# Softmax weights times values: four heads side by side in the array, with value tiles that hold four heads and half of the tokens

## The chip, the cores and the metric

The kernel runs on one core of a Trainium2 chip. The metric is the device time of one execution in microseconds (us). The engines are named as in the profile: PE is the matmul engine and PEld its loads of stationary weights, DVE is VectorE, ACT is ScalarE, POOL is GpSimd, and SP is the queue that issues the DMAs.

## The reference, cut to what matters

Three stages follow each other: a landmark (Nystroem) attention over 4 batches of 8 heads with 576 tokens of 64 elements, a gated MLP, and a mixture of eight experts.

```
def _attn_ref(q, k, v):                      # q, k, v: (4, 8, 576, 64)
    q_lm = q.reshape(B, H, 32, 18, D).mean(axis=3)
    k_lm = k.reshape(B, H, 32, 18, D).mean(axis=3)
    A  = sm(q, k_lm); Bm = sm(q_lm, k_lm); C = sm(q_lm, k)
    Z = ... six Newton steps for the inverse of Bm ...
    return A @ Z @ C @ v
...
x = _moe_ref(attn_out, ...)      # rms norm, silu(x w_gate) * (x w_val), then w_out
return _moe2_ref(x, ...)         # skip score, gate, one expert of eight for each token
```

The change concerns one product, `C @ v`: for each head the 32 x 576 softmax weights of the landmarks times the 576 x 64 values, which gives 32 x 64 numbers for a head.

## The kernel before, in words

**Staging.** `attention(b)` runs once for each batch b = 0 to 3. It handles the 8 heads as two groups `hg` of four heads. A group's 4 x 32 landmark rows fill the 128 partitions, head h in partitions 32h to 32h+31. After the attention of a batch its 576 tokens go through the MLP as two units of 288 tokens (`run_unit`), and the attention of batch b+1 is spread over the units of batch b as a side generator. Batch 0 has nothing to run beside (`fast = True`, own pools with more buffers); there the conversion of the MLP's weights runs between its steps. The experts (`mixture`) come last.

**What sets the order.** The code is written as generators that yield, and a framework orders each engine's instructions from that when the program is built; the order is then fixed. So a small edit can move instructions on all engines. Each engine executes its own row in order, and waits on semaphores. A wait of the first instruction in a row holds up all behind it.

**The product.** In `group`, `load_v` brings values into a tile `vt` with 96 partitions: the 576 tokens are 32 landmarks x 3 thirds t x 6 tokens c, third t goes to partitions 32t to 32t+31, by three DMAs. `cT` holds the transposed softmax weights, 96 x 6 x 128. The product sums six matmuls c = 0 to 5 for each head into partitions 32h to 32h+31 of the PSUM tile `pv`. Its stationary operand is 96 x 32 (one head's weights), its moving operand is 96 x 64 (that head's values). Each such 32-bit float matmul is executed as two passes, so a head takes 12 passes and a group 48. Where four matmuls write to the four different quarters of the partitions, they use four different column tiles of the array (32 columns each). Before the change a value tile holds two heads with all six c, and the matmuls alternate between the two heads of a tile: 24 passes for the first pair of heads, then 24 for the second. For batch 0 both pairs have their own tile. For batches 1 to 3 there is a single `vt` buffer: the second pair's load starts after the first pair's matmuls, and other work stands between the two halves on PE. `A.activation(st["U"][:, hg], pv...)` reads the result.

**Names in rows.** `pv<-vt,cTs` is this product. `pv<-ap_t,P` is another thing: the value half of the MLP's first layer (`gemm`), as `pg<-ap_t,P` is its gate half; `o<-h_t,wo` is the MLP's projection. `P<-w..,WT` are the products that fold the attention's small matrix into the MLP weights (`product`, `product0`), `lp<-x2T,wcat` the logits, `sq<-T,bdq`, `sk<-T,bdk` and `pb<-lmk,bdq` the scores of a group, `bdq`, `bdk`, `T` and `s` what DVE prepares for them. `wo<-s,wo` and `wf` on DVE are conversions of 64-bit weights. `ap_t` is the attention output that the MLP multiplies, and `h` the hidden rows. Line 59 is a helper that all engines' instructions go through; line 248 is the DMA of `load_v`.

Of the kernel before, what the change touches and what calls it, by code (L numbers as in the profile page):

```python
# [6 lines left out]
F32 = mybir.dt.float32  # L7
# [8 lines left out]
B, H, S, D = 4, 8, 576, 64  # L16
# [47 lines left out]
def attention_moe_kernel(  # L64
# [4 lines left out]
    V, A, G, PE = (  # L69
        Paced(e, busy, n)  # L70
        for e, n in (
            (nc.vector, "V"), (nc.scalar, "A"), (nc.gpsimd, "G"), (nc.tensor, "P")
        )
    )
# [3 lines left out]
    def pool(stack, name, bufs=1, **kw):  # L78
        return stack.enter_context(tc.tile_pool(name=name, bufs=bufs, **kw))
# [36 lines left out]
    at = pool(pha, "at", side="right")  # L116
    sm = pool(pha, "sm", side="right")

    start, start1 = ExitStack(), ExitStack()
# [3 lines left out]
    fast = True  # L123
# [7 lines left out]
    def atbank(name):  # L131
        nonlocal nbank
        nbank += 1
        if fast and nbank % 4 < 2:
            return accbank(name)
        if fast and nbank % 4 == 2:
            return bank(name)
        return pa.tile([128, 512], F32, name=name, tag="a")
# [97 lines left out]
        r = st1.tile([128, 2, J * D], F32, name="kq", tag="raw")  # L236
        return {n: load_qk(0, hg, n, r[:, i]) for i, n in enumerate("kq")}

    def load_v(b, h0):
        if fast:  # L240
            vt = st0.tile([96, 2, 6, D], F32, name="vt", bufs=4)
        else:
            vt = at.tile([96, 2, 6, D], F32, name="vt")
        vv = v[b, h0 : h0 + 2].rearrange(
            "h (l t c) d -> t l h (c d)", t=3, c=6
        )
        for t in range(3):
            SP.dma_start(
                vt[32 * t : 32 * t + 32].rearrange("l h c d -> l h (c d)"), vv[t]
            )  # L250
        return vt

# [49 lines left out]
    def group(b, hg, st, loaded=None):  # L302
# [6 lines left out]
        for i, n in enumerate("kq"):  # L309
# [20 lines left out]
                mj.unsqueeze(1).unsqueeze(3).to_broadcast(shape), ALU.mult,  # L330
            )
            yield
        vt = load_v(b, 4 * hg)
        vt1 = load_v(b, 4 * hg + 2) if fast else None

        def two_halves(ps, lhs, rhs):
            for i in range(2):
# [45 lines left out]
        if fast:  # L383
            cT = st0.tile([96, 6, 128], F32, name="cTs", bufs=2)
        else:
            cT = at.tile([96, 6, 128], F32, name="cTs", tag="cG")
# [28 lines left out]
        (G if b in (1, 2) else V).tensor_tensor(eA, eA, b3(arec, L), ALU.mult)  # L415
        yield
        pv = atbank("pv")
        for p in range(2):
            if p:
                vt = vt1 or load_v(b, 4 * hg + 2)  # L420
            for c in range(6):
                for h in (2 * p, 2 * p + 1):
                    PE.matmul(
                        pv[32 * h : 32 * h + 32, 0:D],
                        cT[:, c, 32 * h : 32 * h + 32],
                        vt[:, h % 2, c, :],
                        start=(c == 0), stop=(c == 5),
                    )
        A.activation(st["U"][:, hg], pv[:, 0:D], AF.Copy, scale=crec)

        V.transpose(AT[:, hg], flat(eA))
# [130 lines left out]
    def attention(b, convs=()):  # L562
# [3 lines left out]
        if fast:  # L566
            loaded = [load_fast(hg) for hg in range(2)]
            gs = [group(b, hg, st, loaded[hg]) for hg in range(2)]

            def begin(hg):  # L570
                for _ in range(6):
                    next(gs[hg])
                    yield

            def left(hg):
                yield from inverse(st, hg, 1)

            yield from begin(0)
            ga = chain(begin(1), together(left(1), gs[1]))
            yield from together(ga, left(0), gs[0], convs)  # L580
            lhs, rhs = [st["X", g] for g in range(2)], [U[:, g] for g in range(2)]
        else:
            yield from chain(
                group(b, 0, st), group(b, 1, st), inverse(st, 0, 2, U)
            )
            lhs, rhs = ([st[n, g] for g in range(2)] for n in ("bm", "X"))
# [437 lines left out]
    def pair_at(lst, i):  # L1024
        return ld(lst, i, E - 1), ld(lst, i + LP, B - 1)
# [242 lines left out]
    fast = False  # L1268
# [45 lines left out]
    for u in range(1, 2 * B):  # L1314
        b, half = u // 2, u % 2
# [60 lines left out]
    with tc.For_i(0, npairs) as i:  # L1376
        e, b = pair_at(rest[0], i + 1)
# [36 lines left out]
```

## Time and profile before

| | |
|---|---|
| median of 3 runs | 689.48 us (687.76 to 691.85) |
| profiled execution, its own time | 689.0 us |
| its span (first to last instruction) | 687.3 us |
| mean granted clock of TensorE | 0.962 |
| busy: PE, PEld, DVE, ACT, POOL | 638.6, 552.4, 452.9, 275.1, 146.0 us |
| the product `pv<-vt,cTs` | 384 passes, starts from 23.9 to 389.0 us |

The busy times are of one profiled execution, and the 1.7 us between its span and its own time lie before the first and after the last instruction. An engine's share is an average: PE is nearly always busy after 86 us, and mostly waiting before.

### The profile page before, as it was taken

To read this page: it belongs to the slowest core of one execution; us is meant where nothing else is said; L and a number is where in the kernel's file an instruction comes from. 1 tells how busy PE (TensorE), PEld (TensorE's weight loads), DVE (VectorE), ACT (ScalarE), POOL (GpSimd) and SP (SyncE) were. 2 spreads that over 40 slices of the span, in tenths; PEclk is the share of its full clock that TensorE was granted. 3 is DMA by queue.
4 is the path that set the end of the run, shared out by engine and by line. 5 is a ranking of instruction groups with operands and counts; after the bars stand their busy time and mean duration, and the time that the engine had idled before them with its cause. 6 is when DMAs were issued, how large, how long until landed. Compare 5 with 4: busy or idle time off the path is not lost.

```text
span 687.3 us, 13145 instructions
## 1 busy us (share of the span) xinstructions
PE 638.6 (93%) x4831; PEld 552.4 (80%) x4831; DVE 452.9 (66%) x996; ACT 275.1 (40%) x613; POOL 146.0 (21%) x162
## 2 busy tenths in 40 slices
PE   5677499989999999999999998999999999999997
PEld 5456257977878987979889877999899988988985
DVE  5875899979879767988658867360645446353351
ACT  0652788534234522442531444340543235243240
POOL 4000025504200410320220221040453015032030
PEclk9755789999999999999999999999999999999999
DMA  8578475653249352339442217320552277553454
GB/s 287 197 277 272 178 244 185 199 152 88 53 139 210 74 139 93 62 98 219 102 93 70 70 35 168 98 36 1 152 137 100 43 225 228 163 173 142 138 153 161
DMA packets 111438, 97.16 MB, mean 141 GB/s; under 512 B 50064, under 2 KB 92048, under 8 KB 111376
## 3 DMA queue, kind: packets, MB, share of 16 engines
q1 hardware_dynamic: 111376, 96.34, 49.1%
q8 instruction: 38, 0.62, 0.4%
q14 instruction: 24, 0.20, 0.1%
HBM read 76.97 MB, written 19.34 MB: 140 GB/s over the span
## 4 chain that ended last, share of the span: by engine, by line
PE 66%; DVE 14%; DMA 6%; issue 5%; ACT 5%; POOL 2%; SPq 2%; DVEq 0%; ACTq 0%; POOLq 0%
PE o L59 17%; PE pv L59 10%; PE pg L59 9%; PE ph L59 9%; PE py L59 8%; PE P L59 3%; PE sq L59 2%; DVE wo L59 2%; PE nr L59 2%; PE sk L59 2%; DVE h L59 1%; ACT wo L59 1%; DMA x2r<-xT_d 1%; DVE s L59 1%; DVE T L59 1%
## 5 line engine op out<-in xcount | busy, mean ns | idle before, releaser
L59 PE MATMUL o<-h_t,wo 128*128 128x288 f32 x1152 | 165.9, 299 | 2.3 <-POOL h_t L59 1.4
L59 PEld LDWEIGHTS o<-h_t,wo 128*128 128x128 f32 x1152 | 155.7, 188 | 10.7 <-issue 6.3
L59 POOL TENSOR_TENSOR h_t<-h,h_t 128x288 fp32r<-128x288 f32 x96 | 83.7, 877 | 350.5 <-ACT h_t L59 327.9
L59 PE MATMUL pg<-ap_t,P 128*128 128x288 f32 x576 | 101.1, 304 | 11.1 <-ACT P L59 8.9
L59 PEld LDWEIGHTS pg<-ap_t,P 128*128 128x128 f32 x576 | 82.4, 189 | 25.1 <-issue 18.3
L59 PE MATMUL pv<-ap_t,P 128*128 128x288 f32 x576 | 98.6, 301 | 1.6 <-DVE h L59 1.3
L59 PEld LDWEIGHTS pv<-ap_t,P 128*128 128x128 f32 x576 | 82.7, 188 | 5.3 <-DVE h L59 2.3
L59 PE MATMUL ph<-xsh,P 128*128 128x288 f32 x384 | 78.1, 297 | 0.8 <-DVE P L59 0.8
L59 DVE SCALAR_TENSOR_TENSOR h<-h,pg 128x288 f32<-128x288 f32 x96 | 42.4, 447 | 33.6 <-ACT h L59 33.1
L59 PEld LDWEIGHTS ph<-xsh,P 128*128 128x128 f32 x384 | 62.0, 188 | 1.6 <-ACT P L59 1.0
L59 ACT ACTIVATE h<-pg 128x288 f32<-128x288 f32 x96 | 39.4, 412 | 44.5 <-PE pg L59 44.0
L59 PE MATMUL ph<-xsl,P 128*128 128x288 f32 x192 | 56.8, 296 | 0.0
L59 ACT CAST h_t<-h 128x288 fp32r<-128x288 f32 x96 | 41.2, 431 | 33.9 <-DVE h L59 33.8
L59 PE MATMUL py<-wo,h_t 128*128 128x512 f32 x210 | 51.8, 396 | 0.0
L59 PEld LDWEIGHTS py<-wo,h_t 128*128 128x128 f32 x210 | 39.6, 188 | 9.7
L59 DVE TENSOR_TENSOR h<-h,pv 128x288 f32<-128x288 f32 x96 | 42.5, 447 | 4.8 <-PE pv L59 0.6
L59 DVE STREAM_TRANSPOSE T<-kq 64x576 f32<-64x576 f32 (+1 forms) x40 | 35.5, 888 | 5.7 <-DMA kq<-in_k_dram 4.0
L59 ACT CAST P<-P 128x512 fp32r<-128x512 f32 x48 | 26.6, 586 | 26.9 <-PE P L59 24.9
L59 POOL TENSOR_TENSOR P<-w1r,P 128x512 fp32r<-128x512 f32 x16 | 20.7, 1293 | 74.7 <-ACT P L59 74.7
L59 PEld LDWEIGHTS ph<-xsl,P 128*128 128x128 f32 x192 | 36.2, 188 | 0.1
L59 DVE TENSOR_TENSOR P<-P,P 128x512 fp32r<-128x512 f32 x48 | 31.7, 680 | 4.8 <-ACT P L59 4.7
L59 DVE SCALAR_TENSOR_TENSOR h_t<-ph,h_t 128x288 fp32r<-128x288 f32 (+2 forms) x45 | 14.6, 353 | 28.5 <-ACT h_t L59 28.5
(220 smaller groups left out, 895.6 us busy)
## 6 DMA issues: line engine op xcount, KB each, us to landing
wl<-wg_d SPq DMA_DIRECT2D x36, 256.0 KB, 4.7
wr<-wv_d SPq DMA_DIRECT2D x32, 256.0 KB, 4.9
w1r<-in_moe_w_dram SPq DMA_DIRECT2D x32, 256.0 KB, 3.3
wr<-in_moe_w_gate_dram SPq DMA_DIRECT2D x6, 1024.0 KB, 8.1
wr<-in_moe_w_val_dram SPq DMA_DIRECT2D x6, 1024.0 KB, 5.9
wo<-in_moe_w_dram SPq DMA_DIRECT2D x24, 256.0 KB, 5.2
kq<-in_k_dram SPq DMA_DIRECT2D x8, 576.0 KB, 4.6
kq<-in_q_dram SPq DMA_DIRECT2D x8, 576.0 KB, 4.5
```

The source lines that it names most:

```text
L59: return f(*args, **kw)
```

## The change

The loops over the product are exchanged. All four heads of a group stand in the inner loop, so four consecutive matmuls go to the four column tiles. For batches 1 to 3 a value tile now holds all four heads with three of the six c; it has the same size as before, is still a single buffer, and the second load still follows the first half of the matmuls, now in front of c = 3. Its DMAs copy runs of 192 elements (768 bytes) where there were 384 (1536 bytes), twice as many of them. For batch 0 the tiles stay as they were (two heads each).

```
-    def load_v(b, h0):
+    def load_v(b, hg, i):
         if fast:
             vt = st0.tile([96, 2, 6, D], F32, name="vt", bufs=4)
         else:
-            vt = at.tile([96, 2, 6, D], F32, name="vt")
-        vv = v[b, h0 : h0 + 2].rearrange(
-            "h (l t c) d -> t l h (c d)", t=3, c=6
-        )
+            vt = at.tile([96, 4, 3, D], F32, name="vt")
+        n, m = vt.shape[1], vt.shape[2] * D
+        h0, d0 = (4 * hg + 2 * i, 0) if fast else (4 * hg, m * i)
+        vv = v[b, h0 : h0 + n].rearrange("h (l t c) d -> t l h (c d)", t=3, c=6)
         for t in range(3):
             SP.dma_start(
-                vt[32 * t : 32 * t + 32].rearrange("l h c d -> l h (c d)"), vv[t]
+                vt[32 * t : 32 * t + 32].rearrange("l h c d -> l h (c d)"),
+                vv[t][:, :, d0 : d0 + m],
             )
         return vt
...
-        vt = load_v(b, 4 * hg)
-        vt1 = load_v(b, 4 * hg + 2) if fast else None
+        vt = [load_v(b, hg, i) for i in range(2 if fast else 1)]
...
-        for p in range(2):
-            if p:
-                vt = vt1 or load_v(b, 4 * hg + 2)
-            for c in range(6):
-                for h in (2 * p, 2 * p + 1):
-                    PE.matmul(
-                        pv[32 * h : 32 * h + 32, 0:D],
-                        cT[:, c, 32 * h : 32 * h + 32],
-                        vt[:, h % 2, c, :],
-                        start=(c == 0), stop=(c == 5),
-                    )
+        for c in range(6):
+            if c == 3 and not fast:
+                vt.append(load_v(b, hg, 1))
+            for h in range(4):
+                PE.matmul(
+                    pv[32 * h : 32 * h + 32, 0:D],
+                    cT[:, c, 32 * h : 32 * h + 32],
+                    vt[h // 2][:, h % 2, c] if fast else vt[c // 3][:, h, c % 3],
+                    start=(c == 0), stop=(c == 5),
+                )
```

The framework's order moves with it. A row below counts matmuls, not passes, so a half of a group is x12. The first piece is PE in the second group of batch 0 (lines with - are of before, with + of the change).

```order
 L59 MATMUL nr<-Rb 128x128
-L59 MATMUL pv<-vt,cTs 32x64 x12
+L59 MATMUL pv<-vt,cTs 32x64 x2
 L59 MATMUL nu<-X,Rb 128x32 x2
 L59 MATMUL pG<-U,blk 128x64
 L59 MATMUL nu<-X,Rb 128x32
-L59 MATMUL pv<-vt,cTs 32x64 x12
+L59 MATMUL pv<-vt,cTs 32x64 x22
 L59 MATMUL pG<-U,blk 128x64
```

Of the 24 matmuls, 22 now stand behind the step that half of them stood behind; the two in front are heads 0 and 1 of c = 0.

The second piece is PE where the projection `o` of the first unit ends and the attention of batch 1 begins.

```order
+L59 MATMUL pg<-ap_t,P_662 128x288 x6
+L59 MATMUL pv<-ap_t,P_662 128x288 x3
 L59 MATMUL pb<-lmk_1308,bdq 128x32 x2
 L59 MATMUL sq<-T,bdq 128x288 x4
-L59 MATMUL pg<-ap_t,P_662 128x288 x6
-L59 MATMUL pv<-ap_t,P_662 128x288 x5
```

Nine matmuls of the next MLP unit have moved from behind the scores `pb` and `sq` to in front of them.

The third piece is DVE at the end of batch 0's attention, where the first `ap_t` is made.

```order
 L59 SCALAR_TENSOR_TENSOR wo<-s_839,wo 128x1024
 L59 TENSOR_TENSOR ap<-AT,rbs 128x288 x4
-L59 SCALAR_TENSOR_TENSOR wo<-s_839,wo 128x1024
 L59 TENSOR_TENSOR ap_t<-ap,ap_t 128x288 x4
 L59 TENSOR_TENSOR P_662<-P,P_662 128x512 x2
+L59 SCALAR_TENSOR_TENSOR wo<-s_839,wo 128x1024
 L59 SCALAR_TENSOR_TENSOR wo<-s_918,wo 128x1024
```

One weight conversion has moved from in front of the four `ap_t` rows to behind them and two rows of `P`.

## Rows read from the trace of the kernel before

**Rows 1.** The page, parts 1 and 2: busy times, and TensorE's clock in 40 slices.

```profile
PE 638.6 (93%) x4831; PEld 552.4 (80%) x4831; DVE 452.9 (66%) x996; ACT 275.1 (40%) x613; POOL 146.0 (21%) x162
PEclk9755789999999999999999999999999999999999
```

**Rows 2.** Everything on `vt`: shortest, median and longest pass in ns, then the span of starts.

```profile
L59 PE MATMUL pv<-vt,cTs x384: 218/219/316, 23.9 to 389.0; 96*32 96x64 f32 x192
```

**Rows 3.** Timeline of the product's blocks: start us, length us, engine, group.

```profile
23.90 1.35 PE L59 MATMUL pv<-vt,cTs 96*32 96x64 f32 x48
...
60.95 1.50 PE L59 MATMUL pv<-vt,cTs 96*32 96x64 f32 x24
...
250.15 0.86 PE L59 MATMUL pv<-vt,cTs 96*32 96x64 f32 x24
250.95 7.06 PE L59 MATMUL o<-h_t,wo 128*128 128x288 f32 x51
251.06 1.28 SPq L248 DMA_DIRECT2D vt<-in_v_dram  x3
...
257.94 0.86 PE L59 MATMUL pv<-vt,cTs 96*32 96x64 f32 x24
```

**Rows 4.** `vt` passes in flight in two stretches of 0.20 us, PE and PEld (busy, passes).

```profile
24.15:24.35 0.20, 0.20 (x14) 0.20 (x11) 1.00 0.00 0
24.36:24.56 0.20, 0.20 (x22) 0.20 (x18) 1.00 0.00 0
```

**Rows 5.** A product `P` on eight array tiles: timeline, then the passes' ns.

```profile
226.32 1.09 PE L59 MATMUL P<-wr,WT 64*32 64x256 f32 x32
...
L59 PE MATMUL P<-wr,WT x32: 376/376/400, 226.3 to 227.0; 64*32 64x256 f32 x32
```

**Rows 6.** Busy us (instructions) of PE, PEld, DVE, ACT, POOL by stretch; clock; DMA.

```profile
76.00:86.00 10.00, 1.08 (x6) 0.49 (x2) 10.00 (x13) 6.34 (x11) 0.00 (x0) 0.66 0.82 305
86.00:138.00 52.00, 50.94 (x315) 39.35 (x315) 49.25 (x76) 39.52 (x75) 20.86 (x18) 0.97 0.65 208
145.00:154.00 9.00, 9.00 (x80) 7.32 (x79) 6.35 (x14) 3.61 (x11) 0.79 (x1) 1.00 0.49 130
154.00:182.00 28.00, 25.47 (x219) 21.91 (x218) 26.64 (x74) 10.78 (x32) 9.01 (x10) 1.00 0.33 82
240.00:260.00 20.00, 20.00 (x183) 17.52 (x182) 12.60 (x26) 4.07 (x12) 2.61 (x3) 1.00 0.51 131
267.00:282.00 15.00, 14.64 (x143) 11.70 (x142) 12.50 (x41) 6.21 (x19) 3.53 (x4) 1.00 0.31 78
350.00:380.00 30.00, 30.00 (x259) 25.89 (x258) 22.22 (x58) 7.61 (x24) 1.61 (x2) 1.00 0.34 93
380.00:390.00 10.00, 10.00 (x114) 8.89 (x112) 8.62 (x24) 3.69 (x12) 2.94 (x3) 1.00 0.30 64
```

**Rows 7.** Timeline where DVE and PE wait for each other in batches 1 and 2.

```profile
142.52 0.63 PE L59 MATMUL pb<-lmk,bdq 128*128 128x32 f32 x4 [1.20 <-DVE bdq L59]
...
260.24 0.46 DVE L59 TENSOR_SCALAR x2T<-o 128x288 f32<-128x288 f32 x1 [2.09 <-PE o L59]
...
266.31 0.31 PE L59 MATMUL pb<-lmk,bdq 128*64 128x32 f32 x4 [0.51 <-DVE bdq L59]
```

**Rows 8.** Timeline around the first matmul of the first MLP unit.

```profile
82.77 1.22 DVE L59 SCALAR_TENSOR_TENSOR wo<-s,wo 128x1024 int32<-128x1024 int32 x1
...
83.91 1.56 DVE L59 TENSOR_TENSOR ap_t<-ap,ap_t 128x288 fp32r<-128x288 f32 x4
...
85.42 1.29 DVE L59 TENSOR_TENSOR P<-P,P 128x512 fp32r<-128x512 f32 x2
85.54 0.82 PE L59 MATMUL pg<-ap_t,P 128*128 128x288 f32 x2 [8.92 <-ACT P L59]
```

**Rows 9.** DMA issues between 140 and 400 us: count, size each, median us to landing.

```profile
wr<-wv_d SPq DMA_DIRECT2D x25, 256.0 KB, 4.9
vt<-in_v_dram SPq DMA_DIRECT2D x33, 96.0 KB, 2.3
```

**Rows 10.** The chain that ended last, its piece with the longest DMA before 150 us.

```profile
77.42 6.48 DMA wr<-in_moe_w_val_dram
```

## The prediction, made before the changed kernel was run

> **What bounds the kernel now.** I read the page's busy times first [rows 1]: PE is busy for 638.6 of 687.3 us, and its clock is granted at half in the slices before about 70 us and nearly in full after 100 us. So a matmul that gets shorter can count, but only where PE is what the others wait for. That is read by stretch [rows 6]. From 76 to 86 us PE is idle and DVE busy throughout. From 86 to 138 us both are full: PE 50.94 and DVE 49.25 of 52 us, the weight conversions running beside the first MLP unit. From 154 to 182 us, in the attention of batch 1, DVE is busy 26.64 of 28 us and PE 25.47: DVE leads and PE has the holes. From 240 to 260 (batch 2) and from 350 to 390 us (batch 3) PE has no hole at all.
>
> Then the product itself [rows 2, 3]. It has 384 passes in 8 groups. In batches 1 to 3 that is twelve blocks of 24 passes, each like the two shown, 0.86 us long. A pass takes 219 ns to its end (243 for the first), but passes overlap. A block has 12 rounds of two passes, one for each head of the pair; 0.86 less 0.24 for one pass, over the 11 steps from round to round, is 56 ns a round. At half clock the block of 1.50 us with its longest pass of 0.32 gives 107 ns, twice as much: the round is a number of cycles of this engine.
>
> **The change, step by step.**
>
> *The rounds.* With four heads in the inner loop a block has 6 rounds of four. What such a round takes is the disputed price. From below it is 56 ns: each column tile would still take its own 56 ns. From above it is 112 ns: four passes cost as much as twice two, and nothing is won. The trace holds a piece of the answer, since in batch 0's first group both pairs of heads stand directly behind each other. At two passes a round its 24 rounds would take 23 x 0.056 + 0.24 = 1.53 us; the block takes 1.35 [rows 3]. The time is missing at the change of pairs: a stretch of 0.20 us there has 22 passes in flight, an equal stretch before it 14 [rows 4]. So about three rounds ran with all four column tiles at work. The other near row is a product with eight array tiles [rows 5]: 32 passes of 0.38 us each in 1.09 us, or (1.09 - 0.38)/31 = 23 ns from pass to pass, with 256 columns in each where ours has 64. Issuing and loading weights for a pass therefore costs no more than 23 ns, and four cost at most 92; since those passes are paced by their columns, the real price is lower. I take 56 ns. A block then gets shorter by 6 x 56 = 0.336 us, and the twelve by 4.03 us of PE time. The upper end for issue, 92 ns, would leave 12 x (0.672 - 0.552) = 1.4 us.
>
> The Trainium skill (TensorE: Matmul & The Clock Gate, Part 3, Measured speedup vs the span model) reports 2.38 times the speed for three column tiles, which is 0.79 of full use. By that rule a round of four would cost an estimated 71 ns, and the twelve blocks would give 2.95 us instead of 4.03. With the same share of it kept as below, the result would be an estimated 685.8 us. The trace's stretch with 22 passes against 14 speaks neither clearly for the one nor for the other.
>
> *Batch 0.* The first group's block loses 12 rounds less the three it already saves, about 0.5 us, at 24 us, where PE goes on to wait for DVE and ACT; I count nothing. The second group: the order puts 2 matmuls first and 22 behind the step where the second half stood. Heads 2 and 3 still have 12 passes each in that block, and a column tile takes one a round, so its 12 rounds stay, and with them the 1.50 us. Nothing.
>
> *The transfers.* Three DMAs per load, as before, but with runs of 768 bytes. A load now lands 2.3 us after issue, and the three issues take 1.28 us, so the second half's data are there about 3.6 us after the first half [rows 3, 9]. The second half starts 257.94 - 251.01 = 6.9 us after the first ends, with gemm work in between; the order of the change keeps such work there. The bound from above for landing is that of 256 KB in runs of 1 KB, 4.9 us, which makes 6.2. Still hidden; uncovered by 1 us in each of six groups it would cost 6 us, for PE's row behind it waits.
>
> *What of the 4.03 us stays.* The four blocks of batch 3 lie where PE has no hole: all stays, 1.34 us. The first two of batch 2 lie before the wait of 0.51 us for `bdq` at 266.31. But DVE's work for `bdq` begins with a row that waited 2.09 us for PE's `o` [rows 7], so it comes earlier with PE: 0.67 us stays. Of the last two of batch 2, where DVE is busy 12.50 of 15 us [rows 6], I keep half, 0.34. In batch 1 DVE leads; I keep the last block only, 0.34. Sum 2.69 us, between 1.34 (batch 3 alone) and 4.03.
>
> *Moved work.* Nine matmuls of the next unit now stand before the scores of batch 1. PE was idle there for 1.20 us, waiting for `bdq` [rows 7]. The nine take about nine times 0.13 us (51 `o` passes in 7.06 us, the last one's length included) = 1.2 us, so they fit the hole. The hidden rows that DVE owes for them find room, since DVE is busy only 6.35 of the 9 us from 145 on [rows 6]. I count 1.2 us, between 0 (DVE gives it back by 182) and 1.5.
>
> On DVE the conversion of 1.22 us goes behind `ap_t`, so the first MLP matmul, for which PE sat idle 8.92 us, can start about 1.2 us sooner [rows 8]. But what follows is the stretch in which DVE is full, and its work is the same. I count 0, between 1.2 won and 2.5 lost (the conversion lands 1.22 + 1.29 us later).
>
> Sum: 689.0 - 2.7 - 1.2 = **685.1 us**. This goes against the profiled execution, 0.5 us under the median of the three runs.
>
> **The rivals.** *Absorbed.* The blocks do get shorter, but DVE's stretches and the reshuffled order take all back except batch 3: 689.0 - 1.3 = 687.7 us. For it: PE's holes in 154 to 182 are already larger than what batch 1 saves. Against: 240 to 260 has none.
>
> *No change in the array.* A round of four costs 112 ns. Then only the moved work counts: 689.0 - 1.2 = 687.8 us, or 689.0 without it. Against it stand the 22 passes.
>
> *More.* All twelve blocks count, the whole hole of batch 1 and the 1.2 us at 85 us: 689.0 - 4.0 - 1.5 - 1.2 = 682.3 us.
>
> *Slower: the conversions slip.* The displaced conversion is 2.5 us later on a DVE that is full until 138 us, and behind it stand the stores and the reuse of the raw buffers, whose next transfer was worth 6.48 us on the chain [rows 10]. If one such turn is missed, the first projection waits for its weights: 2.5 + 6.5 = 9.0 us lost against 2.7 won, 695.3 us. It decides from the point where the first scores of batch 1, now at 142.52 us, start more than 2.7 + 3.4 = 6.1 us later. Against it: DVE's total work is unchanged, and its rows go on without a gap.
>
> **How the numbers follow.** I give the forecast 0.50 (own range 683.5, with all twelve blocks and 1.5 us of the hole, to 687.1, with batch 3's blocks and half of the 1.2 us), *more* 0.12, *absorbed* 0.22, *no change in the array* 0.05 and *slower* 0.11. A measurement of this kernel tells about 0.5% from no change, 3.4 us, so faster means below 685.6. That takes in *more* and some two thirds of the forecast's range: 0.12 + 0.33 = 0.45. Slower is 0.11, the rest 0.44. The range goes from *more*, 682.3, to no change at all, 689.0; a little wider at the bottom for batch 0's 0.5 us: 681.8 to 689.0. Outside remain *slower* and a few hundredths.
>
> **What would show it.** A half of a group in batches 1 to 3 should be 0.86 - 0.34 = 0.52 us long, with as many passes; 0.86 would be *no change in the array*, and 0.62 to 0.75 an issue limit. The second block of batch 0 should keep about 1.5 us. PE's wait for `bdq` at the start of batch 1 should be gone, and the batch-1 scores should start within a microsecond of 142.5. The loads of `vt` should land within 2 to 3 us, and no second half should wait for them. The prediction is wrong if DVE's stretch from 154 to 182 us gets longer, or if the conversions end later than before.

## The result, and the profile after

| | before | after |
|---|---|---|
| median of the comparison's runs | 689.31 us (10 runs) | 693.48 us (10 runs) |
| ratio | | 1.0069, 95% interval 1.0045 to 1.0094 |
| span of the profiled execution | 687.3 us | 692.3 us |
| mean granted clock of TensorE | 0.962 | 0.956 |

The change made the kernel 0.7% slower; the forecast was 685.1 us, in a range of 681.8 to 689.0. The profile after shows at once that the array does what was forecast and that something else costs more. First two rows of the page of after.

```profile
PE 638.7 (92%) x4831; PEld 551.9 (80%) x4831; DVE 453.6 (66%) x996; ACT 274.4 (40%) x613; POOL 144.5 (21%) x162
PEclk9755799999999899999999999999999999999999
```

PE's busy time is that of before [rows 1], though its product got shorter, and TensorE's clock has a slice of 8 in the middle of what was a line of nines. The timeline of after, PE and DVE, at the places that the prediction spoke of and at three waits:

```profile
23.47 0.88 PE L59 MATMUL pv<-vt,cTs 96*32 96x64 f32 x48
...
60.69 1.50 PE L59 MATMUL pv<-vt,cTs 96*32 96x64 f32 x44
...
83.88 0.58 PE L59 MATMUL pg<-ap_t,P 128*128 128x288 f32 x1 [7.90 <-ACT P L59]
...
145.85 0.63 PE L59 MATMUL pb<-lmk,bdq 128*128 128x32 f32 x4 [0.41 <-DVE bdq L59]
...
160.10 0.44 DVE L59 SCALAR_TENSOR_TENSOR h<-h,pg 128x288 f32<-128x288 f32 x1
160.46 1.23 DVE L59 TENSOR_TENSOR bdk<-lmk,maskj 128x256 f32<-128x256 f32 x1
161.61 0.77 DVE L59 STREAM_TRANSPOSE AT<-sT 128x576 f32<-128x576 f32 x1
162.31 1.33 DVE L59 STREAM_TRANSPOSE T<-kq 128x1152 f32<-128x1152 f32 x1
163.57 0.41 DVE L59 TENSOR_TENSOR h<-h,pv 128x288 f32<-128x288 f32 x1
164.03 1.07 PE L59 MATMUL pv<-ap_t,P 128*128 128x288 f32 x6 [1.99 <-DVE h L59]
...
183.50 1.16 PE L59 MATMUL pg<-ap_t,P 128*128 128x288 f32 x6 [1.90 <-DVE h L59]
184.59 0.87 PE L59 MATMUL pv<-vt,cTs 96*32 96x64 f32 x24
...
227.85 0.69 PE L59 MATMUL lp<-x2T,wcat 128*32 128x288 f32 x8 [1.43 <-DVE P L59]
...
231.53 1.64 PE L59 MATMUL pg<-ap_t,P 128*128 128x288 f32 x6
...
259.11 0.54 PE L59 MATMUL pv<-vt,cTs 96*32 96x64 f32 x24
```

A half block takes 0.54 us where it took 0.86 [rows 3], and the first MLP matmul starts at 83.88 instead of 85.54 us [rows 8]. But the first scores of batch 1, `pb`, start at 145.85 instead of 142.52 us [rows 7]. PE then stands idle for 1.99, 1.90 and 1.43 us, each time for DVE. And two rows are odd: a half block of 0.87 us at 184.59, and six `pg` passes that take 1.64 us at 231.53, where six take 0.95 elsewhere. The windows around the last two waits say why (columns as in [rows 6], the clock is the eighth):

```profile
181.00:184.30 3.30, 1.40 (x11) 1.16 (x9) 2.65 (x8) 1.15 (x3) 0.51 (x1) 1.00 0.32 55
184.30:187.70 3.40, 3.40 (x37) 2.97 (x36) 2.45 (x6) 1.33 (x4) 2.20 (x3) 0.50 0.35 65
...
226.20:228.70 2.50, 1.07 (x11) 0.39 (x10) 1.60 (x3) 1.76 (x5) 0.79 (x1) 1.00 0.69 136
228.70:235.50 6.80, 6.80 (x31) 6.75 (x31) 3.60 (x13) 2.14 (x8) 1.59 (x2) 0.50 0.20 34
235.50:239.00 3.50, 3.50 (x51) 2.80 (x50) 2.53 (x9) 2.21 (x6) 0.80 (x1) 1.00 0.18 28
```

TensorE was granted half its clock, 1.2 instead of 2.4 GHz, for 3.4 and for 6.8 us, each time soon after one of the waits. Before had no such stretch between 90 and 686 us. Behind the first of the three waits the clock stayed full:

```profile
164.00:167.40 3.40, 3.37 (x22) 2.99 (x23) 3.40 (x9) 1.18 (x3) 1.56 (x2) 1.00 0.58 173
```

The other rows that the prediction named: the loads of `vt`, and DVE's splits of the products `P` from 89 to 122 us.

```profile
vt<-in_v_dram SPq DMA_DIRECT2D x33, 96.0 KB, 2.5
```

```profile
L59 DVE TENSOR_TENSOR P<-P,P 128x512 fp32r<-128x512 f32 x10 | 6.9, 690 | 2.5 <-ACT P L59 2.4
```

The loads land as forecast, in 2.5 us. DVE waited 2.5 us in front of the splits; the same view of before has 0.6 us.

### The profile page after: what moved, and what is told of

It is laid out like the page before. It is cut to its first block, busy times and chain, and to the rows that moved or that the text cites. A ratio compares the mean times of both kernels' runs of the same rounds, so it can differ in the third digit from the quotient of the medians.

```text
span 692.3 us, 13150 instructions
## 1 busy us (share of the span) xinstructions
PE 638.7 (92%) x4831; PEld 551.9 (80%) x4831; DVE 453.6 (66%) x996; ACT 274.4 (40%) x613; POOL 144.5 (21%) x162
## 4 chain that ended last, share of the span: by engine, by line
PE 72%; DVE 14%; DMA 5%; ACT 4%; issue 2%; POOL 1%; SPq 1%; ACTq 0%; POOLq 0%; DVEq 0%
PE o L59 16%; PE py L59 11%; PE ph L59 11%; PE pv L59 9%; PE pg L59 9%; PE P L59 3%; PE sq L59 3%; DVE wo L59 2%; PE nr L59 2%; DMA wl<-wg_d 2%; DVE T L59 2%; PE sk L59 1%; DMA kq<-in_q_dram 1%; DVE h L59 1%; DVE sT L59 1%
## 5 line engine op out<-in xcount | busy, mean ns | idle before, releaser
L59 POOL TENSOR_TENSOR h_t<-h,h_t 128x288 fp32r<-128x288 f32 x96 | 81.7, 854 | 355.1 <-ACT h_t L59 334.5
L59 PE MATMUL pv<-ap_t,P 128*128 128x288 f32 x576 | 102.0, 306 | 2.8 <-DVE h L59 2.8
L59 PEld LDWEIGHTS pg<-ap_t,P 128*128 128x128 f32 x576 | 84.2, 192 | 25.4 <-issue 16.7
L59 PEld LDWEIGHTS pv<-ap_t,P 128*128 128x128 f32 x576 | 84.6, 193 | 8.3 <-DVE h L59 4.0
```

What stands on the lines that cost most here:

```text
L59: return f(*args, **kw)
```

## The experiments

**How a kernel's order is held.** Both kernels write their instructions in the same sequence, up to the operands of one product. So the order in which the framework issues one kernel's rows can be laid on the other: an edge from each row of an engine to the next, which orders them and waits for nothing. The table says it in runs, first number + count, in the order of writing.

```
+ORDER = {
+    'PE': (
+        "0+9 11+5 9+2 16+8 25+2 24 27+10 39+24 37+2 63+3 67 73 66 71+2 68+3 74 76 85 "
...
+        for a, b in zip(want, want[1:]):
+            tc.add_manual_dep(
+                b, a.name,
+                mybir.DependencyInfo(
+                    mybir.DependencyClass.NoSync, mybir.DependencyReason.DATA
+                ),
+                reason="order",
+            )
```

The profiles are compared by three stretches, each from the first start of a matmul to the next, read off the timelines: A from `pG` of batch 0 (about 60 us) to the first `pb` of batch 1, B from there to the projection `o` of unit 2 (about 240 us), C from there to the last matmul. What lies ahead of A differs by up to 4 us between executions of whatever kernel, so this tells more than a single run's time. Each row's stretches are of one profile; in the kernels that were profiled twice, A and B differ by up to 0.9 us and C by up to 0.2. The ratio compares with runs of before in the same comparison, whose medians lie between 687.56 and 689.31 us, so times of different comparisons are compared by the ratio. "New" is the changed kernel's order, "wide" the changed product.

| run | order, product | us | ratio (95%) | A | B | C |
|---|---|---|---|---|---|---|
| before | old, pairs | 689.31 | | 82.66 | 97.36 | 442.41 |
| after | new, wide | 693.48 | 1.0069 (1.0045 to 1.0094) | 86.27 | 102.98 | 438.50 |
| after_again | the same | 693.15 | 1.0080 (1.0052 to 1.0108) | 85.69 | 103.72 | 438.31 |
| wide_oldorder | old, wide | 685.20 | 0.9959 (0.9934 to 0.9984) | 82.13 | 96.53 | 440.10 |
| pairs_neworder | new, pairs | 694.13 | 1.0089 (1.0054 to 1.0124) | 85.79 | 103.57 | 440.24 |
| halves_pairs_oldorder | old, halves in pairs | 686.88 | 0.9995 (0.9965 to 1.0024) | 83.34 | 96.81 | 440.82 |
| early_new | new to 141 us, wide | 690.42 | 1.0024 (0.9998 to 1.0049) | 85.06 | 98.41 | 441.40 |
| batch1_new | new 142 to 209 us, wide | 690.90 | 1.0044 (1.0014 to 1.0074) | 83.31 | 100.65 | 441.34 |
| unit2_new | new 209 to 240 us, wide | 685.45 | 0.9957 (0.9932 to 0.9982) | 82.12 | 96.63 | 439.85 |
| late_new | new from 240 us, wide | 683.81 | 0.9937 (0.9914 to 0.9960) | 82.29 | 96.65 | 438.10 |
| conversion_back | new but 80 to 89 us, wide | 694.85 | 1.0113 (1.0079 to 1.0146) | 86.75 | 100.75 | 438.43 |
| unit0_back | new but 89 to 141 us, wide | 692.18 | 1.0039 (1.0008 to 1.0071) | 83.54 | 103.81 | 437.83 |
| after_filled | new, wide, 1 wait filled | 692.11 | 1.0059 (1.0035 to 1.0084) | 85.45 | 100.77 | 438.29 |
| after_filled3 | new, wide, 3 waits filled | 687.91 | 1.0010 (0.9989 to 1.0031) | 86.02 | 98.95 | 437.92 |
| wide_b23 | framework's own, wide in batches 2 and 3 | 683.25 | 0.9940 (0.9909 to 0.9971) | 82.25 | 97.43 | 438.23 |
| wide_b23_again | the same | 685.87 | 0.9953 (0.9930 to 0.9976) | 83.16 | 97.40 | 438.17 |

### Product and order apart

Theories: *order* (the product gains what was forecast, the order of rows loses it), *tiles* (the new loads or four tiles at once cost), *absorbed*.

**wide_oldorder**: the changed kernel with the table of before.

> The changed passes and loads, with the rows of all five engines held in the order in which the kernel before has them (edges of order only, no waits). Theory 'order': the passes gain what they were forecast to gain and all of the loss is the new order of rows, so this is 685.3 to 686.7 us (2.7 to 4.0 under 689.3), a block is 0.52 us, the clock is granted in full from 90 us on without the two half stretches, and the first scores of batch 1 start within 1 us of 142.5. Theory 'tiles': the 768-byte loads, or four tiles side by side, cost other work time; then it is 692 to 694 us, as after. Theory 'absorbed': 688.5 to 689.3 us, the blocks being shorter but nothing of it left.

**pairs_neworder**: the kernel before with the table of the changed one.

> The passes and loads of the kernel before (heads in pairs), with the rows of all five engines held in the order in which the changed kernel has them. Theory 'order': 696.2 to 697.5 us, that is after's 693.5 plus the 2.7 to 4.0 us that the longer blocks cost; the first scores of batch 1 at about 146 us, and the clock granted at half near 184 and 229 us again. Theory 'tiles': about 689 us, as before, since the order alone costs nothing.

**halves_pairs_oldorder**: the changed tiles and loads, with this loop in batches 1 to 3, old order.

```
-        for c in range(6):
...
+        for i in range(2):
...
+            for p in range(2):
+                for c in range(6) if fast else range(3 * i, 3 * i + 3):
+                    for h in (2 * p, 2 * p + 1):
```

> Order of rows as before; tiles and loads of the change (four heads by half of the tokens), but in batches 1 to 3 within each half the heads in pairs, three rounds of two and three rounds of two, so never four side by side except where the pair changes; batch 0 in pairs as before. If the gain comes from four heads side by side: a half block of about 0.75 to 0.86 us and 688.5 to 689.5 us in all. If it came from the smaller loads or their place: as fast as the run with four side by side, 685 to 687 us. If the loads cost time: over 690 us.

**wide_b23**: old loads and loop in batches 0 and 1, nothing held.

```
+        new = b in (2, 3)
...
+        if new:
...
+        else:
+            for p in range(2):
```

> The change in batches 2 and 3 alone, order left to the framework: rows are as before until the second unit (about 216 us) and differ in about 340 of 3747 rows of TensorE behind it. Theory 'order', with the loss in batch 1 and at 216 to 240 us, where TensorE waits and its clock falls: 686.5 to 688 us (eight blocks of 0.34 us, less what the later rows give back), no half clock near 184 us. If new order costs wherever it comes: 689 to 691 us. Theory 'tiles': 691 to 692 us (two thirds of the loss).

*Order* holds. With the old order the product wins 0.41% of 689 us, 2.8 us (interval 1.1 to 4.5). The order alone, with the old product, costs 0.89%, 6.1 us. The old order's page and three rows of its timeline:

```profile
PE 634.3 (93%) x4831; PEld 547.6 (80%) x4831; DVE 451.9 (66%) x996; ACT 275.0 (40%) x613; POOL 145.8 (21%) x162
PEclk8755889999999999999999999999999999999999
```

```profile
158.06 0.77 DVE L200 STREAM_TRANSPOSE AT<-sT 128x576 f32<-128x576 f32 x1
158.75 0.41 DVE L200 TENSOR_TENSOR h<-h,pv 128x288 f32<-128x288 f32 x1
159.09 1.35 DVE L200 STREAM_TRANSPOSE T<-kq 128x1152 f32<-128x1152 f32 x1
...
230.87 0.97 PE L200 MATMUL pv<-ap_t,P 128*128 128x288 f32 x6
...
249.84 0.54 PE L200 MATMUL pv<-vt,cTs 96*32 96x64 f32 x24
```

PE is busy 4.3 us less than before [rows 1], batch 0's shorter blocks included, and the clock is full from 91 us on. pairs_neworder has the half clock at 184 and 229 us, so it comes with the order and not with the product. Its time came 2 us under the forecast, which had started from after's 693.5 us; in this comparison before, too, was 1.75 us faster than beside after. halves_pairs_oldorder has a surprise. Its half block is shorter than the 0.75 to 0.86 us expected:

```profile
247.62 0.68 PE L200 MATMUL pv<-vt,cTs 96*32 96x64 f32 x24
```

The likely reason: a half has its change of pairs in the middle, where rounds can overlap, as in batch 0 of before [rows 4]. Its stretches add up to 1.5 us less than before's, wide_oldorder's to 3.7 less; in the runs' times it can't be told from before, nor, by the intervals, from wide_oldorder. So in the blocks and stretches the gain goes with how many heads stand side by side, and no cost of the loads shows. wide_b23 came out 3 us faster than expected, and 0.6 us under the range in a second run.

### Where the order loses

Theories: *slip* (the displaced conversion makes DVE late, and what follows is a consequence) and *each place for itself*. The rows of the two orders differ in clusters with the same rows between them, so the table can take a stretch from one kernel and the rest from the other. The first line that each changes in DVE's table, against wide_oldorder's:

```
early_new
-"118+10 156+2 128+2 162 130 132 140 142 163 131 133 141 143 134+2 171 174 136 "
+"118+10 156+2 128+2 162 130 132 140 142 131 133 141 143 134+2 163 171 174 136 "
batch1_new
-"213 221 215 214 216+2 222 218 223 227 219 224 228 225 229 226 230+3 235 233+2 "
+"213 221 215 214 216+2 222 218 223 227 219 224 228 225 229 226 233 230 234 "
unit2_new
-"311+7 342 341 318 320 319 321 344 330 332 345 331 333 349+2 361+2 364 363 365 "
+"311+7 342 341 318 320 319 321 344 330 332 345 331 333 350 349 361+2 364 363 "
late_new
-"446 439 447+3 440 450 461 451+10 475 462+2 476 464 477+2 465 479 466 480+4 487 "
+"446 439 447+3 440 450+5 461 455+6 476+2 462+2 479 464 480+3 475 483 478 465 "
```

Number 163 is the displaced conversion.

> The changed passes; rows of all engines in the changed kernel's order up to about 141 us (batch 0, the first unit with its weight conversions), and behind that in the order of the kernel before. The run that had the old order throughout was 2.8 us faster than before. Theory 'slip' (the displaced conversion makes DVE late, and the rest of the loss follows from that): first scores of batch 1 about 3.3 us later than with the old order, and then most of the later loss too, holes in TensorE behind 160 us and the clock granted at half near 184 and 229 us: 690 to 693 us. Theory 'each place for itself': only the 3.3 us of this stretch, no half clock later: 688 to 689.5 us.

> The changed passes; the changed kernel's order in the attention of batch 1 alone (about 142 to 209 us), the old order ahead of it and behind it. Theory 'slip': the first scores start as with the old order, DVE is not late, and this stretch costs 0 to 1 us: 685 to 686.5 us, no half clock. Theory 'each place for itself': its own rows make the 2.2 us hole at 181 us and the half clock of 3.4 us behind it: 687 to 688 us.

> The changed passes; the changed kernel's order at the start of unit 2 alone (about 209 to 240 us), the old order elsewhere. Theory 'slip': 685 to 686 us, no half clock. Theory 'each place for itself': the order of DVE's rows there (the scaled probabilities of the second half and the split of the product ahead of the hidden rows) makes the hole ahead of the router's product and the half clock of 6.8 us behind it, 3 to 4.4 us: 688 to 690 us.

Neither theory as it stood. The first unit's rows cost A 2.9 us (85.06 against 82.13) and, with one half stretch, B 1.9. Batch 1's rows cost A 1.2 and B 4.1 us, without any slip ahead of them, which speaks against *slip*. Unit 2's rows alone, which *each place for itself* charged 3 to 4.4 us, cost nothing: PE's wait there was 1.11 us and the clock behind it full, where after has 1.43 us and a half stretch. In batch1_new both long waits stand as in after, and each has its half clock (windows of batch1_new):

```profile
158.80:162.10 3.30, 3.26 (x13) 3.26 (x14) 3.30 (x8) 1.17 (x3) 1.92 (x3) 0.50 0.60 179
179.30:182.60 3.30, 3.30 (x35) 2.85 (x35) 2.39 (x7) 1.48 (x4) 2.19 (x3) 0.50 0.32 55
425.10:428.40 3.30, 3.30 (x38) 2.08 (x39) 0.80 (x3) 1.07 (x2) 0.00 (x0) 0.50 0.03 8
```

The third lies in C, where the order is the old one; early_new has such a stretch at 427 us too. Both have a C some 1.3 us longer than wide_oldorder's, which has none there.

The first wait can be read in the DVE rows of after above. Between two rows of the MLP's hidden part, `h`, stand `bdk`, `AT` and `T<-kq`, 3.3 us of the attention's work, and PE waits for the second `h`. In the old order an `h` stands between `AT` and `T<-kq`.

**conversion_back** and **unit0_back**: the changed kernel in its own order, but for one stretch. The first changes a line each for DVE, ACT and SP; DVE's, and the first of the second's:

```
conversion_back
-"118+10 156+2 128+2 162 130 132 140 142 131 133 141 143 134+2 163 171 174 136 "
+"118+10 156+2 128+2 162 130 132 140 142 163 131 133 141 143 134+2 171 174 136 "
unit0_back
-"172 137 175 144 146 145 147 158 176 148 150 149 151 159+2 177 161 164 166 165 "
+"172 137 175 144 146 145 147 176 148 177 149+2 158 151 159 182 195 160 183 161 "
```

> The changed kernel in its own order but for one place: between 80 and 89 us the rows are as before, that is the weight conversion of DVE that had been moved behind the scaled probabilities is in front of them again (7 rows of DVE, 2 of ACT and 2 of the DMA queue in another place; no other row). Theory 'slip': the first scores of batch 1 start within 1 us of where they do with the old order, which gives back about 3 us of the changed kernel's loss: 689.5 to 691 us; the holes of batch 1's own rows at 161 and 181 us stay, with the half clock behind them. If the later rows of the first unit are the cause (94 to 141 us, where the order differs too): the first scores stay 3 us late and the time stays at 693 to 694 us.

> The changed kernel in its own order but for the stretch from 89 to 141 us (first MLP unit and the conversions of the output weights), where the rows of all engines are as before; the displaced conversion at 82 us stays displaced. With that conversion put back alone the first scores stayed late (4.6 us against the scores' place in the run with the old order, counted from the last product of batch 0; the changed kernel 4.1), so it wasn't the cause. If the rows of this stretch are, where DVE has the splits of the products early and waits 2.5 us for ACT's copies instead of 0.8: the first scores start within 1.5 us of the old order's, DVE's wait is 0.8 to 1.2 us again, and the time is 689.5 to 691.5 us, the waits at 161, 181 and 226 us with the half clock behind them still there (mean clock 0.955 to 0.957). If neither place alone is the cause, the first scores stay 3 us or more late and the time is 692.5 to 694.5 us.

With the displaced conversion back in its place nothing is won: A is 86.75 us. *Slip* has fallen. With the rows of 89 to 141 us back, A is 83.54, some 2.5 us less, and DVE's wait in front of the splits is 1.4 us instead of 2.5 (expected 0.8 to 1.2). So that stretch as a whole costs A the most; that it does so by DVE's wait fits but was not tested by itself. A still has 1.4 us over 82.13, and had 1.2 when batch 1's rows alone were new. The time, expected at 689.5 to 691.5 us, came to 692.18.

**late_new**:

> The changed passes; the old order of rows up to about 240 us, the changed kernel's order behind it. In the profiles so far the stretch from the projection of unit 2 to the end takes 440.1 us in the run with the old order throughout and 437.8 to 438.5 us in those with the new order, so the account of the loss closes only if the new order wins about 2 us there. If it does: 682.8 to 684 us, 0.5 to 0.7% faster than before plus what is won, ratio about 0.992, and full clock from 90 us on. If those 2 us were only the return of what was late before: 685 to 686 us, as with the old order throughout.

> The change in batches 2 and 3 alone, in the framework's own order, once more, on the chip of the other run: 683 to 684.5 us, ratio 0.993 to 0.996. It stands beside the run with the new order behind 240 us, which has four heads side by side in batch 1 too (four blocks of 0.32 us, 1.3 us at most): if that counts there, it is 0.5 to 1 us slower than that run.

From 240 us on the new order is better, C 438.10 against 440.10, and with the old product too, 440.24 (pairs_neworder) against 442.41. So the loss adds up: after against wide_oldorder is +4.1 in A, +6.5 in B, and -1.6 in C. late_new has the lowest ratio of all. wide_b23_again, on the same chip, came to 685.87 us, above what was expected, but the two intervals overlap, so the four blocks of batch 1 can't be told apart that way.

### What the half clock costs

**after_filled** and **after_filled3**: matmuls that nobody needs, in front of the instruction that waits. The first has the 11 of unit 2 alone; both keep the changed kernel's order otherwise.

```
+FILL = {(1, 5): 33, (2, 1): 11}
...
+            if (u, f) in FILL:
...
+                for i in range(FILL[u, f]):
+                    PE.eng.matmul(
+                        spare[:, 0:NH], ptile("g", 0, q)[0][:, 0:128],
+                        ap_t[:, u % 2, 0, 0], start=True, stop=True,
+                    )
```

> The changed kernel in its own order, with 11 matmuls of 0.13 us more (a product of the MLP computed again into a spare bank and not used) on TensorE ahead of the router's product in unit 2, where TensorE stood idle for 1.43 us at 226.4 us. If the half clock from 228.7 us follows from this idle time, it is gone or shorter, and up to 3.4 us (6.83 us at half speed) come back: 690 to 692.5 us, against 693.5. If the stretch is bound by DVE's late rows and not by the clock: 693 to 694 us, with full clock and new holes. If the idle time has nothing to do with it, the half stretch stays and the time is 693.5 to 695.

> The changed kernel in its own order, with TensorE kept at work in three of its waits: 17 matmuls more in the wait of 2.3 us at 161.8 us, 16 in that of 2.2 us at 181.3 and 11 in that of 1.7 us at 226.1 (products of the MLP computed again into a spare bank and not used). With the third wait alone filled, the half clock at 229 us was gone in the profile, but another half stretch stood behind the first wait, and the mean clock over the runs hardly rose (0.957 against 0.956). Theory 'clock' (a wait of TensorE of some 2 us can be followed by a stretch at half clock, and these stretches are a large part of the loss): no half stretch between 90 and 400 us, a mean clock of 0.962 to 0.964 as with the old order, and 3 to 4.5 us less than the changed kernel in this same comparison: 689 to 690.5 us. Theory 'DVE' (the time is bound by DVE's late rows, the clock only follows): full clock, but as long as the changed kernel within 1 us.

> The changed kernel itself once more, on the chip of the other two runs of this comparison: 692.5 to 694.5 us, first scores about 3.3 us later than before, mean clock over the runs 0.955 to 0.957, with half stretches behind some of the waits at 161, 181 and 226 us.

With one wait filled the half clock at 229 us was gone and B lost 2.2 us against after, yet the time hardly changed; in its profile the other two waits each had a half stretch. This run alone shows little, for in conversion_back the same wait, not filled, was followed by full clock as well (row of its timeline, then a window):

```profile
229.68 0.69 PE L200 MATMUL lp<-x2T,wcat 128*32 128x288 f32 x8 [1.44 <-DVE P L200]
...
230.00:233.40 3.40, 3.40 (x31) 3.04 (x24) 2.68 (x8) 1.49 (x6) 0.81 (x1) 1.00 0.01 3
```

With three waits filled there was no half stretch, and the kernel took 687.91 us against 693.15 on the same chip: 44 useless matmuls made it 5.2 us faster, more than the 3 to 4.5 expected. The mean clock over the runs rose from 0.954 to 0.964. Timeline of after_filled3 at the second and behind the third wait:

```profile
178.92 2.29 PE L1352 MATMUL spare<-ap_t,P 128*128 128x288 f32 x16
181.05 1.00 PE L202 MATMUL pg<-ap_t,P 128*128 128x288 f32 x6
181.98 0.54 PE L202 MATMUL pv<-vt,cTs 96*32 96x64 f32 x24
...
227.63 0.95 PE L202 MATMUL pv<-ap_t,P 128*128 128x288 f32 x6
228.41 0.96 PE L202 MATMUL pg<-ap_t,P 128*128 128x288 f32 x6
```

The block that took 0.87 us takes 0.54, six passes take 0.96 instead of 1.64. *Clock* holds and *DVE* doesn't. B says the same across the runs that have the new order and the wide product in it: 103.72 and 103.81 us with 13.6 us at half clock (after_again, unit0_back), 102.98 with 10.2 (after), 100.75 and 100.77 with 6.8 (conversion_back, after_filled), 98.95 with none. With 6.8 us it is the same whether the third wait was filled or not. The waits themselves, filled but not shorter, account at most for what B still has over wide_oldorder, 2.4 us.

## Why the prediction was wrong

**The rounds: right.** 0.54 us where 0.52 was forecast; (0.54 - 0.24) over five steps is 60 ns a round of four. Twelve blocks lose 12 x 0.32 = 3.8 us of PE time, 4.03 were forecast. The Trainium skill's three column tiles (TensorE: Matmul & The Clock Gate, Part 3, Measured speedup vs the span model) had given an estimated 71 ns; the trace is nearer to full use. **What stays of it: not contradicted.** 2.8 us against 2.69, but the interval, 1.1 to 4.5, also takes in both bounds of that sum, 1.34 and 4.03; that the middle was hit is partly luck. In wide_oldorder's profile C, which holds batches 2 and 3, is 2.3 us shorter than before's, against 0.67 + 0.34 + 1.34.

**Batch 0 and the transfers: right.** The first block lost 0.47 us, the block of 44 passes took 1.50; the loads landed in 2.5 us and none was waited for.

**Moved work: this step failed.** It put the new order at a win of 1.2 us, for the nine MLP matmuls in front of `pb`, and at nothing for DVE's conversion; the order alone, with the old product, loses 6.1 us (pairs_neworder). The nine did not fit the hole. In wide_oldorder and in batch1_new the same ten `o` matmuls stand ahead:

```profile
140.26 1.59 PE L200 MATMUL o<-h_t,wo 128*128 128x288 f32 x10 [0.88 <-DVE wo L200]
143.05 0.63 PE L200 MATMUL pb<-lmk,bdq 128*128 128x32 f32 x4 [1.21 <-DVE bdq L200]
...
137.25 1.59 PE L201 MATMUL o<-h_t,wo 128*128 128x288 f32 x10 [0.88 <-DVE wo L201]
139.23 1.07 PE L201 MATMUL pg<-ap_t,P 128*128 128x288 f32 x6 [0.39 <-DVE x2T L201]
140.13 0.56 PE L201 MATMUL pv<-ap_t,P 128*128 128x288 f32 x3
140.65 0.63 PE L201 MATMUL pb<-lmk,bdq 128*128 128x32 f32 x4
```

PE waits for `x2T`, the nine take 1.4 us, and the scores start 3.40 instead of 2.79 us behind the `o` rows, 0.6 us later; the other 0.6 us of A's 1.2 lies ahead, where the rows are the same, and is within what two profiles differ by. The displaced conversion itself was harmless, and the first MLP matmul did start sooner, as forecast. What the step left out was larger than what it priced. It took two or three moved pieces for the whole. Yet between 89 and 141 us all five engines' rows stand in another order, with DVE's splits ahead of ACT's copies that they need; and in batch 1 a hidden row behind a transposition. The sentence that DVE's "rows go on without a gap" was wrong by 1.9 us of waiting. One of the prediction's own signs of being wrong came true: the conversions end later, the last one (`wo<-x,wo` on DVE) starting at 141.91 instead of 139.04 us.

**A cost that stood nowhere.** The prediction took the clock for settled from 100 us on. But a wait of 1.3 to 2 us of PE can be followed by half clock for what comes next. Filling the three waits was worth about 5.2 us, on a chip on which the whole loss was 5.3 (693.15 against 687.84).

**The rivals.** *Slower: the conversions slip* had the place and the sign, 3.33 us at `pb`, but not the mechanism: neither the displaced conversion nor a missed transfer made it, and its point of decision, 6.1 us, was never reached. *No change in the array* is out: a half block takes 0.54 us. *Absorbed* was right that the new order takes back what the blocks win, but it left batch 3's 1.3 us standing, and the order took more than everything.

So the account is: product -2.8 us; order +6.1 us with the old product and +7.6 us with the new one (1.0069 less 0.9959, in us of 689), or +9.0 in the stretches of one profile each; of this some 4 to 5 us is clock (B of after and after_again against after_filled3). What stays open is how the rows of 89 to 141 us delay the scores in detail, and why the framework, for an edit that changes no count of instructions, chose another order already in the first 140 us; nothing here shows it.

## What to carry to other kernels

Where a framework orders the rows, an edit is two changes: price the edit with the old order held, and the new order with the old code. Holding one kernel's order on the other took one table for each and told in two runs which of the two it was. And look at the longest waits of the matmul engine, not only at their sum: what a wait costs includes the slower clock behind it, and work of no use in its place can be faster than none.

## What was not expected of the hardware

Half clock came behind waits of 2 us and less, in a program that keeps PE at work before and after them. The shortest was 1.27 us, ahead of the half stretch at 425 us in batch1_new (first row; the second is of before, where full clock followed):

```profile
424.14 0.93 PE L201 MATMUL o<-h_t,wo 128*128 128x288 f32 x5 [1.27 <-POOL h_t L201]
...
424.37 0.93 PE L59 MATMUL o<-h_t,wo 128*128 128x288 f32 x5 [1.36 <-POOL h_t L59]
```

In after the wait of 1.99 us at 162 us was followed by full clock, those of 1.90 and 1.43 us by half. In a second execution of the same program, after_again, all three had it:

```profile
163.70:167.00 3.30, 3.30 (x16) 3.30 (x15) 3.30 (x11) 0.84 (x2) 1.60 (x2) 0.50 0.59 179
184.10:187.50 3.40, 3.40 (x36) 2.95 (x35) 2.58 (x6) 1.46 (x4) 2.33 (x3) 0.50 0.37 71
228.50:235.20 6.70, 6.70 (x30) 6.65 (x31) 3.38 (x11) 2.24 (x8) 1.59 (x2) 0.50 0.20 34
```

So the same wait costs more in one execution than in the next; B is 0.7 us longer in this one. The Trainium skill (TensorE: Matmul & The Clock Gate, Part 1, What's actually happening) says that the clock follows how busy the array has been; the trace agrees in that 0.50 was granted in every one of the three rows above, each behind a wait of PE, but why the wait of 1.99 us brought it in one execution and not in the other is not shown.
